# Opening of an attention and gated FFN kernel: another order, per-chunk loads, and pooling moved between TensorE and VectorE

## Chip, cores and metric

The kernel runs on one core of a Trainium2 chip. The metric is device microseconds of one execution; before the change three runs took 1026.32, 1027.2 and 1026.94 us (median 1026.94).

## What is computed

Four images (B = 4) of 384 x 32 positions and 128 channels. The reference pools kv by 4 x 4 pixels, projects it, attends to it with q, and sends the result through a gated feed-forward layer without biases:

```python
kv_pool = kv.reshape(B, H // r, r, W // r, r, C).mean(axis=(2, 4))   # r = 4
k = v = kv_pool.reshape(B, -1, C) @ w_sr                             # 768 keys an image
a = softmax(q @ k.T / sqrt(C))
x = (a @ v).reshape(B * S, D)                                        # 49152 rows of 128
out = (np.maximum(x @ w_gate, 0) * (x @ w_val)) @ w_out              # d_ff = 1536
```

## The kernel before

**Tiles and stages.** The rows of q are cut into 96 tiles of 512 (24 an image). An image has 768 pooled keys, in six chunks of 128. For each tile TensorE (PE) computes scores against the six chunks, ScalarE (ACT) their exponentials, PE the values, then for each of twelve blocks of 128 hidden columns a value projection and a gate projection, which ScalarE and VectorE (DVE) turn into one block of h, and an output projection. The softmax's row sums are applied last: since the layer has no bias, the output is scaled by the square of the reciprocal sums.

**Two parts in time.** The loop over k (L719) runs tiles through a pipeline, with the order of the engines' work written out by hand as lists of words: FIRST for the first two rounds, STEADY, DRAIN and LAST. Ahead of it stands the opening, the list OPENING (L70), which must pool and project image 0's keys, make the attention of tiles 0 to 3 and the hidden layer of tile 0. Nothing reorders the words: every engine gets its instructions in the order of the list, and waits where an operand or a buffer isn't ready.

**Words of the opening** (j is a chunk, k a tile, n a hidden block):

- a, b, c j (L628): add lines of chunk j's pixels, 128 x 512 fp32, as SUMS (L98) says: a adds two loaded lines, b and c add a third and fourth to the sum. p j (L632) halves the sum to 256 wide.
- T j.part (L637 to turn_add, L270): transposes on PE by an identity matrix, 128 x 128 each, all summed in one PSUM bank of chunk j. A loaded line (parts 0 to 3) has four, part p has two.
- kvT j (L276) copies that bank out, pj j (L284) projects it, key j (L286) stores keys, vt j (L295) and val j (L298) make and store their transpose, the values.
- cast k, qt k, qT k (L184, L190, L193): q tile k cast to fp16, transposed on PE, copied out. qT4 and qT5 are transposing DMAs on the SP queue (L197).
- S k.j (L344): scores of tile k against chunk j, and at once their exponential on ScalarE (L345), called E below. V k.j (L418): values added up in tile k's bank. xT k (L425): that bank copied out, once its six V are in.
- U, R (L432, L440): row sums of tiles 0 to 3 and their reciprocal and square; sixteen small GpSimd (POOL) copies spread the squares (L447).
- v n and g n (L455, L468): projections of tile 0, each followed at once by its consumer: the copy of the value (L462, called y) and the gating on VectorE (L476, called h), which multiplies the value by the positive part of the gate.
- gate, W, wo: GpSimd waits for a line, then starts the loads of the FFN weights; wo also loads the rest of q's second group.

ENGINES (L66) says on which engine a copy or add runs: a for ScalarE, p for GpSimd, else VectorE.

**PSUM banks** are handed out round about, eight in the opening and six for its last eight words; an operation that wants a bank waits for the last reader of that bank.

**Loads.** SP issues, in order (L592 to L600): chunks 0 and 1 (pair 0, four lines of 512 KB; ScalarE issues two of them), w_sr, q tiles 0 and 1, pair 1's line 0, q tiles 2 and 3, pair 1's other lines, pair 2's four lines (chunks 4 and 5), and q tiles 5 and 4 in four pieces of 64 KB each. Eight DMA semaphores go round: a DMA is issued when the one eight before it has landed.

**What opens the loop.** FIRST begins `r v1 o0 v8 v10 o1`: a value projection of tile 1, then the output projection of tile 0's hidden block 0 (o0, L496), which reads what h0.0 wrote. ScalarE's exponentials of the loop are L364; a-turns are transposing DMAs on SP (L391); GpSimd loads the next group of q after the opening (L699, L144). Before the first transposes PE runs a fill of five fp32 matmuls (L615, two passes each).

The functions that the change touches:

Of the kernel before, what the change touches and what calls it, by code (L numbers as in the profile page):

```python
# [9 lines left out]
FP32 = mybir.dt.float32  # L10
FP16 = mybir.dt.float16
AF = mybir.ActivationFunctionType
ALU = mybir.AluOpType
# [3 lines left out]
def kernel(  # L17
# [48 lines left out]
    ENGINES = dict(word.split(":") for word in """  # L66
        key0:a val0:a a1:p kvT1:a key1:a val1:a key2:a val2:a a3:p b3:p p3:p kvT3:a val3:a
        cast0:a cast1:a qT1:a cast3:a cast4:p cast5:p xT1:a xT3:a
    """.split())
    OPENING = """  # L70
        T0.1 T1.3 cast1 T0.3 cast0 T1.2 T0.2 a1 p1 T1.p T0.0 kvT1 kvT0 pj1 qt1 pj0 T2.0 qT1 a3
        key1 cast3 qt0 cast2 vt1 qT0 key0 S1.1 qt2 qt3 qT2 val1 qT3 S1.0 S0.1 T2.1 S0.0 vt0 val0
        V1.1 S2.0 b3 c3 S2.1 S3.0 S3.1 T2.2 V0.1 T2.3 V1.0 kvT2 V2.1 V0.0 p3 gate22 W0 W1 cast4
        qT4 wo cast5 qT5 pj2 V2.0 T3.p T5.0 key2 vt2 kvT3 val2 pj3 key3 S0.2 T5.1 vt3 val3 S2.3
        a4 S0.3 S1.2 S2.2 T5.2 V0.2 S3.2 b4 V2.3 T5.3 V0.3 c4 S1.3 kvT5 S3.3 pj5 p4 T4.p V1.2
        key5 kvT4 V1.3 S0.5 pj4 key4 S2.5 vt5 val5 V2.2 S0.4 vt4 val4 S2.4 V0.5 V3.0 S1.4 V0.4
        S3.4 xT0 S1.5 V2.5 V2.4 S3.5 xT2 v0.5 g0.5 U0 v0.2 U1 v0.0 R g0.2 v0.3 V1.4 V3.1 g0.0
        v0.1 v0.4 V1.5 g0.3 v0.9 v0.11 g0.4 g0.9 V3.4 v0.8 v0.10 g0.1 xT1 g0.8 V3.5 v0.7 g0.11
        V3.3 v0.6 V3.2 g0.10 xT3 g0.7 g0.6
    """.split()  # L80
    LAST = [f"{head}{n}" for n in range(NFB) for head in "ovygh"] + ["oT"]
    FIRST = """
# [14 lines left out]
    """.split()  # L97
    SUMS = [{}, {"a": [0, 1]}, {}, {"a": [0, 1], "b": ["s", 2], "c": ["s", 3]}, {"a": [0, 1], "b": ["s", 2], "c": ["s", 3]}, {}]  # L98

# [16 lines left out]
    def freed(ps):  # L116
        free_banks.append(bank_numbers.pop(id(ps))[0])
        return ps
# [90 lines left out]

    def kv_load(b, pair, lines=range(r), queues=(nc.sync,)):  # L210
# [12 lines left out]
        rows = kv[b, pair * 2 * HC : (pair + 1) * 2 * HC].rearrange(  # L223
            "(hp dh) (wp h dw) c -> dh hp wp (h dw c)", dh=r, h=2, dw=r
        )
        for dh in lines:
            queues[dh % len(queues)].dma_start(
                parts[dh].rearrange("p h dw c -> p (h dw c)"), rows[dh]
            )

# [16 lines left out]
    def line(chunk, dh):  # L247
        return kv_in[0, chunk // 2][dh][:, chunk % 2]
# [3 lines left out]
    def add(name, to, x, y):  # L252
        engine_of(name).tensor_tensor(to, x, y, op=ALU.add)
# [6 lines left out]
    def sum_pixels(name, chunk):  # L260
        s1 = sums.pop(chunk)
        pixels[chunk] = work.tile([128, 2, C], FP32, tag="kv_c2", bufs=2, name="kv_c2")
        add(name, pixels[chunk], s1[:, 0:2], s1[:, 2:4])

    def turn_add(chunk, lines):
# [72 lines left out]
    hTs, o_banks, o_sbs, vals = {}, {}, {}, {}  # L338

    def scores(k, jc):  # L340
        if k not in aTs:
            aTs[k] = work.tile([128, NJC, T], FP16, tag="aT", bufs=AT_BUFS, name="aT")
        s_ps = bank([128, T])
        nc.tensor.matmul(s_ps, kv16[:, k // NST, jc, 0:C], qT_of(k), start=True, stop=True)  # L344
        nc.scalar.activation(aTs[k][:, jc, :], freed(s_ps), AF.Exp, scale=qk_scale)  # L345

# [79 lines left out]

    def lead_sums(chunks):
        if "sums" not in x_banks:
            x_banks["sums"] = bank([128, T])
        for jc in chunks:  # L430
            for k in range(LEAD):
                nc.tensor.matmul(  # L432
                    x_banks["sums"][32 * k : 32 * (k + 1), :], ones, aTs[k][:, jc, :],
                    start=jc == 0, stop=jc == NJC - 1, skip_group_check=True,
                    tile_position=(0, 32 * k),
                )

    def lead_scales():
# [21 lines left out]
    def keep_value(k, fb):  # L460
        vals[k, fb] = work.tile([128, T], FP16, tag="val", bufs=6, name="val")
        (nc.vector.tensor_copy if k < LEAD - 1 and fb == 5 else nc.scalar.copy)(  # L462
            vals[k, fb], freed(proj_banks.pop(("v", k, fb)))
        )
# [125 lines left out]

    w_sr_f32 = const.tile([128, C], FP32)
    kv_load(0, 0, range(r), (nc.sync, nc.scalar))  # L592
    nc.sync.dma_start(w_sr_f32, w_sr)
    q_load_pair(0)
    kv_load(0, 1, range(1))
    q_load_pair(2)
    kv_load(0, 1, range(1, 4))
    kv_load(0, 2)
    q_load_tile(5)
    q_load_tile(4)  # L600

# [16 lines left out]

    fill(5)
    freed(idle)  # L620

    gate = const.tile([128, 1], FP32)
    done = set()

    def open_step(word):
        head = "T" if word[0] == "T" else word.rstrip("0123456789.")
        at = [int(x) for x in word[len(head):].split(".") if x] if head != "T" else []
        if head in ("a", "b", "c"):  # L628
# [5 lines left out]
        elif head == "r":  # L634
            c2 = pixels[at[0]]
            add(word, c2[:, 0], c2[:, 0], c2[:, 1])
        elif head == "T":  # L637
            j, part = word[1:].split(".")
            turn_add(
                int(j), line(int(j), int(part)) if part.isdigit() else  # L640
                pixels.pop(int(j))[:, 0 : 2 if part == "p" else 1],
            )
# [16 lines left out]
        elif head == "S":  # L659
            scores(*at)  # L660
            done.add(tuple(at))
        elif head == "V" and at[0] < LEAD:
# [3 lines left out]
        elif head == "U":  # L666
            lead_sums(range(at[0] * (NJC - 1), NJC - 1 + at[0]))
        elif head == "R":
            lead_scales()
        elif head == "v":  # L670
            value_proj(*at)
            keep_value(*at)
        elif head == "g":
            gate_proj(*at)
            gated(*at)
        elif head == "W":
# [19 lines left out]
    for at, word in enumerate(OPENING):  # L696
        usable[0] = 8 if at < len(OPENING) - 8 else 6
        open_step(word)
# [110 lines left out]
```

## Time and profile before

| | us |
|---|---|
| median of three runs | 1026.94 |
| span of the profiled execution | 1024.5 |
| PE busy | 1019.4 |
| ScalarE busy | 919.9 |
| VectorE busy | 861.8 |
| GpSimd busy | 524.8 |
| first transpose of pixels starts | 8.07 |
| first projection of keys starts (L284) | 11.69 |
| first and last exponential of the opening start | 13.77, 28.23 |
| first output matmul, o0 (L496), starts | 36.66 |

The span is that of one execution under the profiler, from its first to its last instruction; that execution's own time beyond the span isn't listed, so the median stands 2.4 us above it. Times below are counted from the span's start. A line of the timeline gives start, duration, engine, source line and operation, what it writes and reads, how many instructions were merged (x), and in brackets the engine's idle time before and what ended it.

### The profile page before, as it was taken

The page shows a single profiled execution, that of the slowest core. Times are in us where ns is not written, and L with a number is a line of the kernel's source. Part 1 is how long each engine was busy: PE and PEld are TensorE (multiplying, and loading weights), DVE is VectorE, ACT ScalarE, POOL GpSimd, SP SyncE. Part 2 cuts the span into 40 slices and gives each one's busy share as a digit, 9 for nine tenths or more (in the row PEclk, how much of TensorE's full clock was granted, in tenths as well). Part 3 has the DMA queues.
Part 4 walks back from the last instruction along what each step waited for, and adds up shares of the span by engine and source line. Part 5 has one row for each costly group of instructions (what it writes and reads, how often), then busy time and mean ns, then how long its engine had stood idle before and what let it go on. Part 6 is the DMA issues. An engine that isn't in the chain of part 4 may idle for free.

```text
span 1024.5 us, 17514 instructions
## 1 busy us (share of the span) xinstructions
PE 1019.4 (100%) x5048; PEld 489.5 (48%) x5048; DVE 861.8 (84%) x1432; ACT 919.9 (90%) x1931; POOL 524.8 (51%) x1308
## 2 busy tenths in 40 slices
PE   9999999999999999999999999999999999999998
PEld 5444444444444444444444444444444444444445
DVE  2888888888888888888888888888888888888888
ACT  5999999989999999899999999989999999999986
POOL 3588857344346586544434856654333543343342
DMA  9999999877998999869879899887686987867541
GB/s 330 159 173 184 176 183 159 151 131 120 139 184 168 189 186 164 143 115 146 128 126 211 160 180 194 157 138 134 118 139 108 145 134 119 129 115 123 102 87 45
DMA packets 475312, 153.49 MB, mean 150 GB/s; under 512 B 451536, under 2 KB 465360, under 8 KB 475216
## 3 DMA queue, kind: packets, MB, share of 16 engines
q1 hardware_dynamic: 453184, 126.08, 67.7%
q0 software_dynamic: 21600, 25.19, 15.9%
q10 hardware_dynamic: 432, 1.11, 0.3%
q8 instruction: 40, 0.66, 0.3%
q14 instruction: 56, 0.46, 0.1%
HBM read 53.94 MB, written 26.35 MB: 78 GB/s over the span
## 4 chain that ended last, share of the span: by engine, by line
PE 98%; DMA 1%; ACT 1%; SPq 0%; issue 0%
PE bank_ps L455 24%; PE bank_ps L468 24%; PE bank_ps L496 23%; PE bank_ps L401 12%; PE wide_ps L359 12%; DMA q<-in_q_dram 1%; PE bank_ps L482 1%; PE bank_ps L344 1%; PE bank_ps L418 1%; PE bank_ps L270 0%; PE wide_ps L302 0%; PE bank_ps L284 0%; ACT a L364 0%; ACT val L462 0%; PE bank_ps L432 0%
## 5 line engine op out<-in xcount | busy, mean ns | idle before, releaser
L476 DVE SCALAR_TENSOR_TENSOR hT<-bank_ps,val 128x512 f16<-128x512 f32 x1152 | 727.8, 680 | 105.4 <-PE bank_ps L468 83.7
L462 ACT CAST val<-bank_ps 128x512 f16<-128x512 f32 x1149 | 628.1, 595 | 45.4 <-PE bank_ps L455 24.9
L455 PE MATMUL bank_ps<-xT,wv 128*128 128x512 f16 x1152 | 420.5, 379 | 0.0
L468 PE MATMUL bank_ps<-xT,wg 128*128 128x512 f16 x1152 | 375.9, 379 | 0.0
L496 PE MATMUL bank_ps<-hT,wo 128*128 128x512 f16 x1116 | 348.4, 379 | 0.0
L364 ACT ACTIVATE a<-wide_ps 128x768 f16<-128x768 f32 x368 | 302.0, 821 | 44.0 <-PE wide_ps L359 43.9
L359 PE MATMUL wide_ps<-kv,qT 128*128 128x512 f16 x736 | 179.7, 326 | 0.1
L401 PE MATMUL bank_ps<-aT,kv 128*128 128x512 f16 x552 | 178.9, 379 | 0.0
L496 PEld LDWEIGHTS <-wo 128*128 128x128 f16 x1116 | 109.2, 98 | 131.9 <-issue 0.6
L468 PEld LDWEIGHTS <-wg 128*128 128x128 f16 x1152 | 112.7, 98 | 122.4 <-issue 0.2
L509 POOL TENSOR_TENSOR o_sb<-o_t,scale 128x512 f32<-128x512 f32 x89 | 93.2, 1047 | 145.9 <-issue 128.4
L455 PEld LDWEIGHTS <-wv 128*128 128x128 f16 x1152 | 112.7, 98 | 105.7 <-issue 1.2
L385 POOL COPY scale<-square 32x8 f32<-32x8 f32 x736 | 141.2, 192 | 28.6
L739 POOL DMA_DIRECT2D out_dram<-o_sb x216 | 134.8, 627 | 19.5 <-POOL o_sb L509 13.0
L378 POOL TENSOR_TENSOR square<-inverse 128x8 f32<-128x8 f32 x46 | 9.3, 202 | 255.6 <-DVE inverse L376 249.4
L359 PEld LDWEIGHTS <-qT 128*128 128x128 f16 x736 | 72.0, 98 | 87.1 <-issue 0.4
L409 DVE CAST xT<-bank_ps 128x512 f16<-128x512 f32 x92 | 63.6, 691 | 32.0 <-PE bank_ps L401 32.0
L401 PEld LDWEIGHTS <-kv 128*128 128x128 f16 x552 | 54.0, 98 | 65.1
L364 ACT ACTIVATION_READ_ACCUMULATOR a<-wide_ps 128x1 f32 x368 | 75.9, 206 | 0.0
L504 DVE STREAM_TRANSPOSE o_t<-bank_ps 128x512 f32<-128x512 f32 x93 | 65.4, 703 | 0.0
L144 POOL DMA_DIRECT2D q<-in_q_dram x84 | 46.7, 573 | 0.6 <-PE bank_ps L496 0.4
L237 POOL TENSOR_TENSOR s<-kv_in 128x512 f32<-128x512 f32 x36 | 45.1, 1284 | 0.7
(78 smaller groups left out, 204.9 us busy)
## 6 DMA issues: line engine op xcount, KB each, us to landing
kv_in<-in_kv_dram SPq DMA_DIRECT2D x42, 512.0 KB, 4.7
out_dram<-o_sb SPq DMA_DIRECT2D x177, 64.0 KB, 3.7
out_dram<-o_sb POOLq DMA_DIRECT2D x176, 64.0 KB, 4.2
q<-in_q_dram POOLq DMA_DIRECT2D x84, 128.0 KB, 5.8
aT<-a SPq DMA_TRANSPOSE x184, 4.3
kv_line<-in_kv_dram SPq DMA_DIRECT2D x4, 512.0 KB, 9.7
placed<-blocks SPq DMA_DIRECT2D x9, 128.0 KB, 2.7
kvT<-placed SPq DMA_DIRECT2D x36, 32.0 KB, 2.1
```

What stands on the lines that cost most here:

```text
L359: nc.tensor.matmul(s_ps[:, j0 * 128 : j1 * 128], qT, kv16[:, b, j0:j1, 0:C], start=True, stop=True)
L364: nc.scalar.activation(a16s[k][:, s, :], s_banks.pop(s)[:, 0:J], AF.Exp, scale=qk_scale, accum_out=a_sums[k // 2][:, k % 2, s : s + 1],)
L385: nc.gpsimd.tensor_copy(to[32 * b : 32 * (b + 1), :, :, j], squares[k // 2][32 * j : 32 * (j + 1)])
L401: nc.tensor.matmul(x_banks[k], kv16[:, k // NST, jc, C : 2 * C], aT[:, jc], start=first, stop=x_left[k] == 0,)
L455: nc.tensor.matmul(proj_banks["v", k, fb], wv16[:, fb * 128 : (fb + 1) * 128], xTs[k], start=True, stop=True,)
L462: (nc.vector.tensor_copy if k < LEAD - 1 and fb == 5 else nc.scalar.copy)(vals[k, fb], freed(proj_banks.pop(("v", k, fb))))
L468: nc.tensor.matmul(proj_banks["g", k, fb], wg16[:, fb * 128 : (fb + 1) * 128], xTs[k], start=True, stop=True,)
L476: nc.vector.scalar_tensor_tensor(hTs[k][:, fb, :], freed(proj_banks.pop(("g", k, fb))), 0.0, vals.pop((k, fb)), op0=ALU.max, op1=ALU.mult,)
L496: nc.tensor.matmul(o_banks[k], wo16[:, fb, :], hTs[k][:, fb, :], start=fb == 0, stop=fb == NFB - 1)
L504: nc.vector.transpose(o_t, freed(o_banks.pop(k)))
L509: nc.gpsimd.tensor_tensor(to, o_by, scale.to_broadcast([128, NS, 4, 32]), op=ALU.mult)
L739: queue.dma_start(*out_moves.pop())
```

## The change

Only the opening is changed; FIRST, STEADY, DRAIN and LAST stay.

1. **Loads.** The order is a list, LOADS. It is the same up to pair 2, whose four lines become eight loads of 256 KB: first chunk 4's half of each line, then chunk 5's.
2. **Pooling.** A new word, d j.part, sums the four neighbouring pixels of a line or of a sum with one tensor_reduce on VectorE (512 to 128 wide). Chunks 0 and 3 are wholly added up (a, b, c) and reduced; PE then has a single transpose for each (T j.ds). Chunk 4 has its line 2 and its sum of lines 0 and 1 reduced (d2, ds) and line 3 transposed. Chunk 1's sum goes to PE unreduced (T1.s). In all PE has 36 such transposes instead of 62.
3. **Order.** Scores and exponentials, projections and their consumers are words of their own (S and E, v and y, g and h), and the list is written anew. The row sums U come in one run near the end, R after them; cast4, qT4, wo, cast5 and qT5 stand just before R. The list ends with `R g0.4 y0.4 h0.4 h0.0`.
4. **Smaller things.** Other engines for some copies and adds; the square of R on GpSimd; the value copy that VectorE takes for tile 0 is block 2's; the fill has three matmuls; six banks hold for the last twelve words.

```diff
+        a0 a1 T1.s b0 T1.2 T1.3 kvT1 c0 pj1 cast1 cast0 d0.s key1 qt1 qt0 qT1 T0.ds vt1 kvT0
+        qT0 S1.1 pj0 val1 E1.1 S0.1 key0 cast3 V1.1 E0.1 vt0 cast2 S0.0 qt3 val0 E0.0 V0.1 qt2
+        a2 S1.0 qT3 V0.0 qT2 a3 S3.0 S3.1 E3.0 p2 S2.0 T2.2 b3 E3.1 T2.p S2.1 E2.0 T2.3 c3 E2.1
+        V3.1 E1.0 V2.0 kvT2 V2.1 d3.s pj2 V1.0 a4 V3.0 key2 T3.ds vt2 S0.2 kvT3 S3.2 val2 E0.2
+        pj3 d4.2 S2.2 key3 T4.3 d4.s E3.2 T4.d2 S1.3 E2.2 T4.ds vt3 V3.2 a5 kvT4 gate21 W0 W1
+        V0.2 E1.3 S3.3 pj4 val3 V2.2 E3.3 b5 V1.3 S2.3 key4 S0.3 p5 vt4 E2.3 T5.3 E0.3 T5.p
+        S1.4 V2.3 kvT5 val4 S2.4 E1.4 pj5 S0.4 E2.4 V0.3 key5 V1.4 E0.4 S0.5 S2.5 vt5 E0.5 V2.4
+        S1.5 val5 V0.4 E2.5 V0.5 S3.5 E1.5 S3.4 xT0 V2.5 E3.5 S1.2 V1.5 xT2 v0.2 E1.2 v0.5 v0.3
+        y0.2 E3.4 g0.2 g0.5 y0.5 V3.5 h0.2 V3.4 v0.1 y0.3 v0.11 h0.5 g0.3 y0.1 g0.1 v0.10 h0.3
+        y0.11 g0.10 g0.11 V1.2 h0.1 y0.10 v0.6 g0.9 xT1 h0.11 g0.6 v0.9 y0.6 V3.3 h0.10 v0.7
+        y0.9 v0.8 v0.0 h0.6 g0.7 y0.8 g0.8 h0.9 y0.7 U1 U4 U3 y0.0 h0.8 U2 U0 xT3 U5 h0.7 v0.4
+        g0.0 cast4 qT4 wo cast5 qT5 R g0.4 y0.4 h0.4 h0.0
...
+    LOADS = "P0 w Q0 P1.0 Q2 P1.1 P1.2 P1.3 K4 K5 q5 q4".split()
...
+            if half is not None:
+                own = slice(half * r * C, (half + 1) * r * C)
+                to, line_rows = to[:, own], line_rows[:, :, own]
...
+    def reduce_pixels(chunk, part):
+        lines = sums.pop(chunk) if part == "s" else line(chunk, int(part))
+        reduced[chunk, part] = work.tile([128, 1, C], FP32, tag="kv_d", bufs=4, name="kv_d")
+        nc.vector.tensor_reduce(
+            reduced[chunk, part][:, 0], lines.rearrange("p w c -> p c w"),
+            axis=mybir.AxisListType.X, op=ALU.add,
+        )
...
-        nc.scalar.activation(aTs[k][:, jc, :], freed(s_ps), AF.Exp, scale=qk_scale)
+
+    def exponentials(k, jc):
+        nc.scalar.activation(
+            aTs[k][:, jc, :], freed(score_ps.pop((k, jc))), AF.Exp, scale=qk_scale
+        )
...
-        nc.vector.tensor_tensor(square, inverse, inverse, op=ALU.mult)
+        nc.gpsimd.tensor_tensor(square, inverse, inverse, op=ALU.mult)
...
-    fill(5)
+    fill(3)
```

On GpSimd are now b0, a4, cast0, cast2, cast4 and cast5; on ScalarE cast1, kvT0, kvT4, key0 to key4, val4, qT2, qT3, xT1 and xT3; the rest of such words on VectorE.

More of the change, by code (lines that the diff above doesn't have):

```diff
@@ L73 @@
[L73 to L78, printed above, removed]
@@ L208, with kv_load @@
     kv_in = {}
-    def kv_load(b, pair, lines=range(r), queues=(nc.sync,)):
+    def kv_load(b, pair, lines=range(r), queues=(nc.sync,), half=None):
         if (b, pair) not in kv_in:
@@ L425, in lead_kept, with lead_sums @@
         copy_on(name, xTs[k], freed(x_banks.pop(k)))
-    def lead_sums(chunks):
+    def lead_sums(jc):
         if "sums" not in x_banks:
[L429 to L436, printed above, removed]
+            x_banks["sums"], x_count["sums"] = bank([128, T]), 0
+        x_count["sums"] += 1
+        for k in range(LEAD):
+            nc.tensor.matmul(
+                x_banks["sums"][32 * k : 32 * (k + 1), :], ones, aTs[k][:, jc, :],
+                start=x_count["sums"] == 1, stop=x_count["sums"] == NJC, skip_group_check=True,
+                tile_position=(0, 32 * k),
+            )
     def lead_scales():
@@ L636, in open_step @@
             add(word, c2[:, 0], c2[:, 0], c2[:, 1])
+        elif head == "d":
+            j, part = word[1:].split(".")
+            reduce_pixels(int(j), part)
         elif head == "T":
@@ L640, in open_step @@
                 int(j), line(int(j), int(part)) if part.isdigit() else
+                sums.pop(int(j)) if part == "s" else
+                reduced.pop((int(j), part[1:])) if part[0] == "d" else
                 pixels.pop(int(j))[:, 0 : 2 if part == "p" else 1],
@@ L660, in open_step @@
             scores(*at)
-            done.add(tuple(at))
+        elif head == "E":
+            exponentials(*at)
         elif head == "V" and at[0] < LEAD:
```

61 lines of the change are left out of this document (30 added, 31 removed).

## Prediction

> **What bounds the kernel now.** I read the chain of waits first, then the busy time after the opening, then PE, ScalarE and VectorE in order of time up to 38 us.
>
> ```profile
> PE 98%; DMA 1%; ACT 1%; SPq 0%; issue 0%
> ```
>
> The chain that ends last is matmuls nearly from end to end. In the windows view (PE's busy time is the second number), the stretch from 36.70 us on reads:
>
> ```profile
> 36.70:1024.50 987.80, 984.48 (x4846) 469.55 (x4844) 845.38 (x1397) 895.76 (x1880) 508.88 (x1267) 1.00 0.84 146
> ```
>
> Matmuls there start 0.216 us apart (512 columns); only twice does one start over 0.1 us late, 0.27 us at 54.8 and 0.18 at 424.7. So the loop has 0.45 us to give back, and the end moves with the first output matmul o0 (L496), which opens it:
>
> ```profile
> 36.44 0.38 PE L455 MATMUL bank_ps<-xT,wv 128*128 128x512 f16 x1
> 36.66 0.38 PE L496 MATMUL bank_ps<-hT,wo 128*128 128x512 f16 x1
> ```
>
> What o0 needs is made by VectorE (first fence) and ScalarE (second), here from about 25 us:
>
> ```profile
> 26.96 0.69 DVE L128 CAST xT<-bank_ps 128x512 f16<-128x512 f32 x1 [0.85 <-PE bank_ps L418]
> 27.83 0.69 DVE L128 CAST xT<-bank_ps 128x512 f16<-128x512 f32 x1 [0.17 <-PE bank_ps L418]
> 28.43 0.68 DVE L462 CAST val<-bank_ps 128x512 f16<-128x512 f32 x1
> 29.23 0.69 DVE L476 SCALAR_TENSOR_TENSOR hT<-bank_ps,val 128x512 f16<-128x512 f32 x1
> 30.36 0.72 DVE L440 STREAM_TRANSPOSE sums_turned<-bank_ps 128x512 f32<-128x512 f32 x1 [0.44 <-PE bank_ps L432]
> 31.11 0.25 DVE L442 RECIPROCAL inverse<-sums_turned 128x16 f32<-128x16 f32 x1
> 31.49 6.69 DVE L476 SCALAR_TENSOR_TENSOR hT<-bank_ps,val 128x512 f16<-128x512 f32 x11
> ```
>
> ```profile
> 20.72 3.76 ACT L345 ACTIVATE aT<-bank_ps 128x512 f16<-128x512 f32 x7
> 24.83 4.05 ACT L345 ACTIVATE aT<-bank_ps 128x512 f16<-128x512 f32 x8 [0.34 <-PE bank_ps L344]
> 29.99 1.73 ACT L462 CAST val<-bank_ps 128x512 f16<-128x512 f32 x3 [1.12 <-PE bank_ps L455]
> ```
>
> VectorE ends its twelve gatings at 38.18, 1.5 us after o0, without harm: h0.0, the one that o0 reads, was early in the list. ScalarE ends its exponentials at 28.87, then idles 1.12 us while PE runs row sums. The first question is where the new list puts h0.0.
>
> **The change, part by part.** Pitches from rows (start to start): an exponential or a value copy on ScalarE 0.48, a small ScalarE copy 0.17, gating on VectorE 0.60, a 512-wide fp32 add on VectorE 0.69 (0.72 when it needs the one before), a 128-wide copy there 0.29, a transpose group of four 0.44 plus 0.17 to its result.
>
> *Loads.* Eleven DMAs up to the second pair's last line are issued as before; that line is issued at 8.67 and lands 8.0 later, 16.7. Then four 512 KB loads become eight of 256 KB, 2 KB a partition. SP issues each when the DMA eight before has landed, the last at 16.7, so SP isn't late. The last full line landed at 22.2:
>
> ```profile
> kv_line<-in_kv_dram SPq DMA_DIRECT2D x1, 512.0 KB, 10.6
> ```
>
> Price: 512 KB landed every 1.28 us before it, so 2 MB at that pace ends at 21.85. The nearest 2 KB row is the late q loads (64 KB, 32 partitions): five land from 22.45 to 23.43, 0.245 us each; at that rate a half takes 0.98 us and the eighth lands at 24.6. I take 22.2: same source and same 128 partitions as the full lines. The Trainium skill, DMA: Bandwidth & Descriptors, section Specifications, asks only 512 B a transfer for line rate, which would give 21.85; the q row disagrees, and no run shows halves yet. Behind the halves on SP the late q loads are issued from about 17.4 on (12.9 before), but the last of the eight waits, as before, for the last line, 22.2: so cast4 (27.17), wo (issued 27.73, landed 33.17) and qT4 stay, all before o0. Without that cover, o0 would wait for wo one for one.
>
> *PE.* Transposes fall from 62 to 36: 26 x 0.109 = 2.8 us less. Of the fill, four of ten passes go (0.43 each); the first transposes then wait for two adds on VectorE after line 0 (landed 6.22), 7.7 instead of 8.07. PE is nearly idle from 6.4 to 11. The fill's passes are 0.85 us apart until 5.8 and 0.43 after; should half rate return, PE's 2.4 us of work from 10.3 to 14.3 runs some 0.9 late, which ScalarE's idle spots below (1.3 us by 19.2) take up. I cost it at nothing; without that cover it is the 0.9.
>
> *VectorE.* It has four wide adds now; it gets nine and four reductions: 5 x 0.69 + 4 x 0.69 = 6.2 us more, put into its long waits (3.27, 2.14, 2.00 us before its L128, L253 and L291 instructions). A reduction of 512 to 128 isn't in the trace: at least the 0.43 of a 512-wide cast between buffers, at most the 1.27 of GpSimd's add. I take 0.69, as the adds, which read as many elements on this engine. The Trainium skill, VectorE: DVE Perf Modes, section The perf-mode tier table, has it at one element a cycle in every type, like the fp32 add; by that the sum is the one below, by the cast's row it is rival (2), and no run here shows it yet.
>
> **The new path to o0.** From 16.7 VectorE carries one chain: c3 0.72, kvT2 0.31, reduction d3 0.70, out to PE and back 0.35, kvT3 0.29, val2 0.25, reductions d4.2 and d4.s 0.72 each, 0.05 of semaphore: 4.1, so 20.8. T4.ds on PE and its wait, 0.35: ScalarE starts kvT4 at 21.2. Ahead of E0.5 ScalarE has three small copies (0.51), seven exponentials (3.36) and about 0.3 of waits for scores: E0.5 runs 25.36 to 25.95. PE sums V0.5 (0.53 with V0.4 in front), and xT0 starts at 26.5, 0.46 earlier than now. ScalarE starts exponentials 1.2 us sooner (12.6 against 13.77), but that is lost: it idles 0.5 and 0.76 us between 17.7 and 19.2 and 0.33 before kvT4.
>
> From xT0 VectorE has two xT and y0.2 (3 x 0.61), twelve gatings (12 x 0.60), the row sums' transpose and reciprocal (1.04; the square goes to GpSimd), 0.3 for y0.2's result and the last one's tail: 10.4. ScalarE is no longer in its way: its value copies run from 28.3 (29.99 now), the 1.12 us gap is gone, and all end by 35.2. So VectorE ends at 36.9 against 38.18. But h0.0 is now the last of the list, behind the row sums: o0, second in the loop's list, waits for it until 36.95. PE, done with the opening at about 34.9, stands for 2 us.
>
> **Sum:** 36.95 - 36.66 = +0.3 us. Backlogs of ScalarE and VectorE at o0 are smaller, which can return at most the 0.27 at 54.8; I leave it. Span 1024.8 against 1024.5. The median of the runs shown lies 2.4 above that span; same offset: **1027.2 us**, no change that counts. (A measurement of this kernel tells about 0.2%, 2.05 us, from no change.)
>
> The sums' late place also moves GpSimd: its sixteen scale copies (31.64 to 35.29 now) run from 35.8 to 39.6 and hold the next q load (issued 37.08, last landing 44.15 now) to 39.9, landing about 47.0. SP's transpose of it starts at 48.24 now; 1.2 us of cover hide it. Gone, that transpose would hold the stores and a-turns behind it on SP.
>
> **Rivals.** (1) *Slower: the halves land late.* T5.3, the last line's transpose, stands in PE's queue from 22.8, with S1.4, V2.3 and all later matmuls behind it. A last half later than 22.8 delays everything one for one; at 24.6, 1.8 us: +2.1, **1029.1**. For: the q row. Against: 32 partitions aren't 128, and full lines ran 1.28 us to the end.
> (2) *A little faster.* Reductions at 0.43 shorten the chain by 3 x 0.26; T5.3 then waits for the landing: -0.6 on the path, **1026.6**. The floor is the landing at 21.85 with nothing else late: T5.3 and T5.p (0.85), kvT5 (0.35), pj5 (0.45), key5 (0.3) and S0.5 (0.45) put E0.5 at about 24.25, 1.1 earlier, and o0 at 35.8: **1026.1**. Over 2 us isn't in reach.
> (3) *Reductions at 1.27*, by their strided read: 3 x 0.58 = +1.7, **1028.9**.
> (4) *It doesn't do what it says:* chunks 0 and 3 do reach PE as one transpose each; that fewer transposes buy nothing is the forecast itself.
>
> **How the numbers follow.** Forecast 0.57, (1) 0.17, (2) 0.14, (3) 0.07, a wait that I missed 0.05. The range takes in the bounds of the unknown prices, with some 0.2 below the floor for the runs' own spread (0.9 here): 1025.9 to 1029.1. Slower by over 0.2% (above 1029.0) is half of (1), half of (3) and the missed waits: 0.17. Faster: 0.03. Same: 0.80.
>
> **What would show it.** VectorE's reductions at 0.69; the last half landing by 22.2 to 22.8; xT0 near 26.5; ScalarE going from exponentials to value copies without a gap; the last opening gating ending at about 36.9, and PE idle some 2 us just before the first output matmul. Wrong if that matmul starts clearly before 36, if the loop shows stalls that it lacks now, or if 512-wide matmuls still stand 0.43 us apart past 16 us.

## The result, and the profile after

| us | before | after |
|---|---|---|
| median of 20 runs | 1026.81 | 1028.38 |
| lowest and highest of them | 1026.23, 1027.56 | 1027.31, 1034.09 |
| span of the profiled execution | 1024.5 | 1032.3 |
| first output matmul, o0, starts | 36.66 | 37.76 |
| from o0 to the end of the span | 987.9 | 994.5 |

The ratio is 1.002, 95% interval 1.0013 to 1.0026: the changed kernel is about 0.2% slower. The forecast was 1027.2, in a range of 1025.9 to 1029.1. The median lies in the range and 1.2 us above the forecast, and the new runs are spread over 6.8 us where the old ones had 1.3. So there are two questions: why o0 starts later than forecast, and where the spread comes from. The profiled execution is the slowest of the 20 (1034.09 us) and shows both.

The chain of waits of the changed kernel, which was 98% PE and 1% DMA:

```profile
PE 94%; DMA 4%; DVE 1%; ACT 1%; issue 0%; DVEq 0%
```

The stretch from o0 on, in the windows view (columns: stretch, its length, then busy time and count of PE, its weight loads, VectorE, ScalarE and GpSimd; then clock, DMA share, GB/s):

```profile
37.76:1032.30 994.54, 986.33 (x4845) 469.90 (x4844) 844.56 (x1394) 896.15 (x1878) 511.49 (x1280) 1.00 0.84 145
```

Before, this stretch took 987.80 with 984.48 of it busy. Here it has 6.7 us more, so most of this execution's loss lies *behind* the opening that was changed. PE in order of time shows two waits in it, each in front of a value product (L423) for a transposed block of exponentials that a DMA on SP brings:

```profile
114.22 0.38 PE L477 MATMUL bank_ps<-xT,wv 128*128 128x512 f16 x1
115.94 0.38 PE L423 MATMUL bank_ps<-aT,kv 128*128 128x512 f16 x1 [1.33 <-DMA aT<-a]
...
178.77 0.38 PE L477 MATMUL bank_ps<-xT,wv 128*128 128x512 f16 x1
182.45 0.59 PE L423 MATMUL bank_ps<-aT,kv 128*128 128x512 f16 x1 [3.30 <-DMA aT<-a]
```

The idle time in brackets counts from the modelled end of the matmul before, so what is lost is the distance of the starts less 0.216: 1.5 and 3.5 us. The second wait is followed by 3.42 us at half the clock, which costs 1.7 more:

```profile
182.44:185.86 3.42, 3.41 (x9) 1.33 (x10) 1.38 (x2) 1.34 (x3) 0.00 (x0) 0.50 1.46 170
```

1.5 + 3.5 + 1.7 = 6.7, all that the stretch has more. The other new executions that were profiled and have no such wait take 987.7 to 988.1 us from o0 to the end, as before. So the time of each profiled run here is the start of o0 plus the waits in the loop, and I follow the two apart.

**The opening.** PE at o0 (first fence; before, o0 followed the projection ahead of it without a gap), then VectorE from the landing of pair 1's last line (16.90) to o0, then ScalarE:

```profile
36.01 0.38 PE L477 MATMUL bank_ps<-xT,wv 128*128 128x512 f16 x1
37.76 0.38 PE L519 MATMUL bank_ps<-hT,wo 128*128 128x512 f16 x1 [1.37 <-DVE hT L499]
```

```profile
16.99 0.69 DVE L259 TENSOR_TENSOR kv_s<-kv_s,kv_in 128x512 f32<-128x512 f32 x1 [0.40 <-DMA kv_in<-in_kv_dram]
17.69 0.29 DVE L132 COPY kvT_chunk<-bank_ps 128x128 f32<-128x128 f32 x1
17.90 1.03 DVE L276 TENSOR_REDUCE kv_d<-kv_s 128x128 f32<-128x512 f32 x1
...
19.70 1.04 DVE L276 TENSOR_REDUCE kv_d<-kv_line 128x128 f32<-128x512 f32 x1
20.65 1.02 DVE L276 TENSOR_REDUCE kv_d<-kv_s 128x128 f32<-128x512 f32 x1
...
27.48 1.34 DVE L132 CAST xT<-bank_ps 128x512 f16<-128x512 f32 x2 [0.64 <-PE bank_ps L440]
28.77 0.69 DVE L485 CAST val<-bank_ps 128x512 f16<-128x512 f32 x1
29.58 6.08 DVE L499 SCALAR_TENSOR_TENSOR hT<-bank_ps,val 128x512 f16<-128x512 f32 x10
35.58 0.71 DVE L462 STREAM_TRANSPOSE sums_turned<-bank_ps 128x512 f32<-128x512 f32 x1
36.32 0.25 DVE L464 RECIPROCAL inverse<-sums_turned 128x16 f32<-128x16 f32 x1
36.49 1.22 DVE L499 SCALAR_TENSOR_TENSOR hT<-bank_ps,val 128x512 f16<-128x512 f32 x2
```

```profile
22.16 0.27 ACT L130 COPY kvT_chunk<-bank_ps 128x128 f32<-128x128 f32 x1 [0.68 <-PE bank_ps L311]
...
24.82 4.61 ACT L365 ACTIVATE aT<-bank_ps 128x512 f16<-128x512 f32 x9
29.31 2.06 ACT L485 CAST val<-bank_ps 128x512 f16<-128x512 f32 x4
```

This is the forecast's chain with another number in it. o0 waits for the gating that is last in the list (ends at 37.71), ScalarE goes from exponentials to value copies without a gap, and the row sums stand between the last gatings. But each reduction takes 1.02 to 1.04 us, where the forecast had 0.69, and kvT4 (22.16 against 21.2), xT0 (27.48 against 26.5) and o0 (37.76 against 36.95) are late by 0.96, 0.98 and 0.81. The line that starts the chain is late too: it landed at 16.90 (forecast 16.7).

Seven of the eight halves landed from 17.57 on, 0.67 to 0.69 apart, and the last 1.27 behind the seventh, at 22.91:

```profile
kv_line<-in_kv_dram SPq DMA_DIRECT2D x8, 256.0 KB, 7.5
```

PE turned the last of them (T5.3) at 23.74; it did not wait for it.

### The profile page after: what moved, and what is told of

It is laid out like the page before. It is cut to its first block, busy times and chain, and to the rows that moved or that the text cites. A ratio compares the mean times of both kernels' runs of the same rounds, so it can differ in the third digit from the quotient of the medians.

```text
span 1032.3 us, 17469 instructions
## 1 busy us (share of the span) xinstructions
PE 1017.6 (99%) x5018; PEld 485.7 (47%) x5018; DVE 868.5 (84%) x1440; ACT 920.6 (89%) x1929; POOL 525.1 (51%) x1309
## 3 DMA queue, kind: packets, MB, share of 16 engines
q10 hardware_dynamic: 432, 1.11, 0.3%
## 4 chain that ended last, share of the span: by engine, by line
PE 94%; DMA 4%; DVE 1%; ACT 1%; issue 0%; DVEq 0%
PE bank_ps L477 24%; PE bank_ps L491 24%; PE bank_ps L519 23%; PE bank_ps L423 12%; PE wide_ps L381 11%; DMA aT<-a 2%; DMA kv_in<-in_kv_dram 1%; PE bank_ps L505 1%; DMA kv_line<-in_kv_dram 1%; DVE hT L499 1%; PE wide_ps L318 0%; PE bank_ps L440 0%; ACT a L386 0%; PE bank_ps L362 0%; ACT val L485 0%
## 5 line engine op out<-in xcount | busy, mean ns | idle before, releaser
L423 PE MATMUL bank_ps<-aT,kv 128*128 128x512 f16 x552 | 179.7, 381 | 4.6 <-DMA aT<-a 4.6
L423 PEld LDWEIGHTS <-kv 128*128 128x128 f16 x552 | 54.2, 98 | 71.1 <-issue 6.7
```

What stands on the lines that cost most here:

```text
L423: nc.tensor.matmul(x_banks[k], kv16[:, k // NST, jc, C : 2 * C], aT[:, jc], start=first, stop=x_left[k] == 0,)
```

## The experiments

**Theory** after reading the two traces: (a) the reductions make o0 about 0.9 us late; (b) the fill of three matmuls instead of five lets TensorE's clock fall back to half in the opening of many executions; (c) the loop's waits come from the late load of q's third group on GpSimd (issued at 41.19, before 37.08) and from SP's in-order transpose of it (49.58, before 48.24). **Rivals:** the halves, or the order of the words, make o0 late; the waits follow from the half clock, or from something in the opening that neither (b) nor (c) names.

How to read the times of many runs, of which only one is profiled: a stretch of 3.41 us at half clock lowers the mean clock of a run by 0.5 x 3.41/1024 = 0.0017, so 0.998 is one such stretch, 0.997 or 0.996 two. As a mark for a wait in the loop I count the runs that lie over 2.0 us above the fastest of the same kernel; half clock in the opening alone made less (e1). It is a mark and no proof: the wait itself is seen only in a profile, a short wait goes unmarked, and e10's two marked runs are just the longest of its five at a clock of 0.998.

| kernel | median, us | lowest, highest | runs with the mark |
|---|---|---|---|
| changed (all above) | 1028.38 | 1027.31, 1034.09 | 2 of 20 |
| e1 changed, again | 1028.88 | 1027.27, 1033.73 | 4 of 10 |
| e2 fill of five | 1027.47 | 1027.19, 1027.86 | 0 of 11 |
| e3 blocks renamed | 1029.36 | 1025.76, 1033.62 | 9 of 12 |
| e4 adds for reductions | 1027.11 | 1026.37, 1034.06 | 1 of 12 |
| e5 renamed, fill of five | 1026.16 | 1025.85, 1030.73 | 2 of 12 |
| e6 as e5, q early | 1025.98 | 1025.82, 1026.42 | 0 of 12 |
| e7 before, fill of three | 1027.17 | 1026.33, 1033.55 | 1 of 12 |
| e8 before, q late | 1027.43 | 1026.24, 1034.71 | 5 of 12 |
| e9 changed, q early | 1030.14 | 1027.42, 1034.04 | 6 of 12 |
| e10 as e6, whole lines | 1027.90 | 1027.09, 1029.38 | 2 of 12 |
| e11 as e6, adds | 1025.43 | 1025.18, 1028.97 | 1 of 12 |
| e12 as e9, fill of five | 1027.62 | 1027.19, 1029.32 | 1 of 11 |
| before, beside e1 to e4 | 1026.85 | 1026.11, 1027.37 | 0 of 33 |
| before, beside e5 to e8 | 1026.84 | 1026.12, 1033.74 | 3 of 35 |
| before, beside e9 to e11 | 1026.83 | 1026.22, 1032.37 | 2 of 29 |
| before, beside e12 | 1026.82 | 1026.28, 1027.43 | 0 of 15 |

The four groups of experiments (e1 to e4, e5 to e8, e9 to e11, e12) ran on different chips, so a kernel is best compared within its group.

### e1: the changed kernel again

> The changed kernel once more, unaltered, for a second profile and for the spread. Theory A (half clock): the runs that are longest by 0.8 to 1.6 us are those whose mean granted clock is under 0.999, since PE now stands nearly idle between about 6 and 11 us; in a profile of such a run the 512-wide matmuls of the opening stand 0.43 us apart for one or two stretches of 3.4 us. Theory B (loop stalls): the long runs are long because a transposing load of the attention weights lands late in the loop, as at 178 us of the first profile, and any half clock comes after such a stall. Both expect a median of about 1028.4; A expects the fastest runs, at clock 1.000, near 1027.4.

Measured: ratio 1.0029 (1.0017 to 1.0042). This profiled execution has no wait in the loop (987.93 us from o0 to the end) but another opening: o0 at 38.64, 0.88 later than in the first profile. The windows view has the reason, the clock (the column behind the engines):

```profile
5.00:7.60 2.60, 0.59 (x2) 0.00 (x0) 1.07 (x2) 0.00 (x0) 0.00 (x0) 1.00 1.03 424
7.60:11.01 3.41, 2.98 (x12) 2.28 (x12) 0.23 (x1) 0.48 (x1) 1.72 (x2) 0.50 1.03 407
```

The same stretch of the first profile, without the half clock:

```profile
7.60:11.01 3.41, 2.22 (x14) 1.57 (x14) 1.01 (x3) 0.50 (x1) 1.74 (x2) 1.00 1.04 410
```

PE has 14 matmuls in 2.22 us of busy time there; at half clock it is through with 12 in 2.98. So kvT1, the copy behind the first transposes, waits longer on VectorE (first profile, then e1), and the sums, scores and exponentials behind it start later:

```profile
10.19 0.29 DVE L132 COPY kvT_chunk<-bank_ps 128x128 f32<-128x128 f32 x1 [2.40 <-PE bank_ps L286]
11.15 0.29 DVE L132 COPY kvT_chunk<-bank_ps 128x128 f32<-128x128 f32 x1 [3.32 <-PE bank_ps L286]
```

The delay reaches o0 whole: xT0 28.36 against 27.48. A late load is not the reason, since pair 1's last line landed at 16.91, and at 16.90 in the first profile. Counted from that landing, the opening's last gating ends after 20.81 to 20.83 us in the five profiles with halves, reductions and full clock (the first, e5, e6, e9, e12), after 21.67 in e1 and 21.55 in e3, the two with half clock; e2 (21.33) has one add of 1.11 us instead of 0.69.

Of the changed kernel's 20 runs, 11 had a clock of 0.998 or less, in one of them (the profiled one) from the stretch behind the loop's wait; the two marked runs left out, those at 0.996 took 1028.99 to 1029.28, those at 0.998 1028.22 to 1028.37, and the lowest at 0.999 or more 1027.31 to 1027.56: some 0.85 us for each stretch. (None with two was profiled. Three unmarked runs at full clock took 1027.96, 1028.40 and 1029.20; what held them isn't known.) The Trainium skill, TensorE: Matmul & The Clock Gate, section What's actually happening, has a window of 3413 ns for the gate that runs free of the kernel, so that the time of a change of clock differs between runs of one kernel; the 3.41 us and the spread agree.

### e2: the fill at five

```diff
-    fill(3)
+    fill(5)
```

> The changed kernel with the fill of before (five matmuls instead of three). Theory A (half clock in the opening): PE is kept busy until about 7.5 us, hardly any run is under clock 0.999, and the median falls by about 0.8 us to 1027.6, with a narrower spread. Theory B (loop stalls): median and spread stay as in the changed kernel, 1028.4 and some 2 us.

Measured: 1027.47, ratio 1.0006 (0.9998 to 1.0015), clock 1.000 or 0.999 in all 11 runs, no mark. So the two matmuls of fill are worth 1.4 us of the median (e1 beside it: 1028.88). In the forecast they were costed at nothing. (The profile's own o0, 38.16, is late by the long add; e12, with the same opening, has 37.51.) The fill covers the hole: with it, PE is busy in the whole of 5.00 to 7.60 (here in e12, whose opening is the same on PE), where e1 had 0.59 us.

```profile
5.00:7.60 2.60, 2.60 (x7) 0.91 (x5) 1.29 (x2) 0.00 (x0) 0.00 (x0) 1.00 1.02 414
```

The traces' clock records change at steps of 3.41 us: in the first profile, 52 of them back from 182.44 is 4.95, and e1's stand at 4.18, 7.60 and 11.01. PE's busy time in the step around the hole, in the first profile and in e1:

```profile
4.95:8.36 3.41, 1.53 (x7) 0.61 (x5) 1.29 (x2) 0.00 (x0) 0.00 (x0) 1.00 1.02 414
4.19:7.60 3.41, 1.40 (x4) 0.32 (x2) 1.07 (x2) 0.00 (x0) 0.00 (x0) 1.00 1.03 423
```

With three matmuls, the next step was at half clock after 1.40, 1.55 and 1.30 us of work (e1, e3, e7) and not after 1.53, 1.75 and 1.84 (the first profile, e4, e9); with five, no step of the profiled openings between 4 and 14 us has under 2.2. So the short fill leaves a step near an edge, which these traces don't place more sharply. Where the steps lie differs from run to run, so a run can go either way: of all stretches of 3.41 us there, the emptiest has 0.98 to 1.75 us of work in the profiles of the new order with three matmuls, and 2.03 or more in those with five (worked out from PE's rows).

### e3: the block that o0 reads is gated first

The blocks of tile 0 are only renamed (2 and 0 change places, and others), so each engine has the same work at the same place:

```diff
-        ... v0.2 E1.2 v0.5 v0.3 y0.2 E3.4 g0.2 ... h0.2 ... R g0.4 y0.4 h0.4 h0.0
+        ... v0.0 E1.2 v0.1 v0.2 y0.0 E3.4 g0.0 ... h0.0 ... R g0.10 y0.10 h0.10 h0.11
```

> The changed kernel with the hidden blocks of tile 0 renamed in the opening, so that the same instructions stand in the same places but the block that the loop's first output matmul reads is the first that VectorE gates and not the last. Theory A (the first output matmul waits for the last gating): that matmul starts right behind the value projection ahead of it, at about 36.2 us instead of 37.8, PE's idle time of 1.4 us there goes, and the time falls by 1.5 us, below the kernel before the change. Theory B (the late path through exponentials and VectorE sets the loop's start whatever block comes last): PE meets the same wait a few matmuls later and the time falls by less than 0.4 us.

Measured: in the profile o0 starts at 36.63, right behind the projection ahead of it, while the last gating ends at 38.11; from o0 on 988.06 us. With the order of the changed kernel o0 would have stood till 38.11 (this execution has half clock from 8.94 to 12.35): the last place of h0.0 costs 1.5 us. It is the forecast's reading of the list, confirmed. In time the lowest run shows it, 1025.76 against 1027.27 in e1. But the median became *longer*, 1029.36, since 9 of 12 runs have the mark. Four of these nine ran at a clock of 1.000, so half clock is no condition of the waits.

### e4: two adds for each reduction

```diff
-        nc.vector.tensor_reduce(reduced..., lines.rearrange("p w c -> p c w"), axis=X, op=add)
+        nc.vector.tensor_tensor(half, lines[:, 0:2], lines[:, 2:4], op=ALU.add)
+        nc.vector.tensor_tensor(reduced..., half[:, 0], half[:, 1], op=ALU.add)
```

> The changed kernel with each tensor_reduce (1.04 us in its profile) replaced by two adds on VectorE, 512 to 256 and 256 to 128 wide, which the profile's rows put at 0.43 and 0.29. Theory A (three of the four reductions stand in the one chain that leads to the loop): each gives 0.32 us, the first xT starts about 0.9 us sooner (26.6 instead of 27.5), and the time falls by 0.8 to 0.9 us, where the landing of the last half line (22.9) begins to bind. Theory B (the exponentials on ScalarE set the start of the first xT): xT moves by less than 0.3 us and the time with it.

Measured: 1027.11, ratio 1.0009 (0.9998 to 1.002). What follows a pair of adds starts 0.72 and 0.66 us after the pair's start (19.42, 20.14, 20.80), about what the forecast had for a reduction; behind the reductions it was 0.95 and 0.94:

```profile
19.42 0.47 DVE L276 TENSOR_TENSOR kv_d<-kv_line 128x256 f32<-128x256 f32 x1
19.93 0.29 DVE L278 TENSOR_TENSOR kv_d<-kv_d 128x128 f32<-128x128 f32 x1
20.14 0.42 DVE L276 TENSOR_TENSOR kv_d<-kv_s 128x256 f32<-128x256 f32 x1
20.59 0.29 DVE L278 TENSOR_TENSOR kv_d<-kv_d 128x128 f32<-128x128 f32 x1
20.80 0.69 DVE L259 TENSOR_TENSOR kv_s<-kv_line 128x512 f32<-128x512 f32 x1
```

and o0 comes out where the forecast put it, 36.96 (forecast 36.95), with the landing that the forecast had for pair 1's last line (16.71), xT0 at 26.68 (26.5) and the same wait in front:

```profile
36.96 0.38 PE L518 MATMUL bank_ps<-hT,wo 128*128 128x512 f16 x1 [1.36 <-DVE hT L498]
```

### e5 and e6: both mends, and then the load of q early

e5 is e3 with the fill at five. e6 is e5 with this:

```diff
-        ... cast5 qT5 R g0.10 y0.10 h0.10 h0.11
+        ... cast5 qT5 q2 R g0.10 y0.10 h0.10 h0.11
...
+        elif head == "q":
+            nc.gpsimd.tensor_copy(gate, hTs[0][:, 9, 0:1])
+            q_load(at[0])
...
-    nc.gpsimd.tensor_copy(gate, hTs[0][:, NFB - 1, 0:1])
-    q_load(2)
```

> The changed kernel with two edits: the blocks of tile 0 renamed so that the block that o0 reads is gated first (as in the run before, alone), and the fill back at five matmuls. Theory (reductions at 1.04 us cost about 0.9, the half clock of the opening another 0.8 in most runs, and waits in the loop come from the late load of q's third group, which here waits for the gating that ends last): no half clock in the opening, o0 at 36.2 to 36.8, clock 1.000 in nearly all runs; but the load of q is issued no earlier than 41.5, so waits in the loop stay in some of the runs, 1026.0 to 1026.6 in those without one and up to several us more in those with one. Rival (the waits in the loop come from the half clock in the opening): none in any run, all within 1026.0 to 1026.8.

> As the kernel before it in this call, and the load of q's third group is issued before the sixteen scale copies on GpSimd, behind the gating of block 9 instead of block 11. Theory: the load is issued at 36 to 37.5 and lands by about 44.5, SP's transpose of it starts at about 48.3 without holding anything, no run has a wait in the loop: 1025.8 to 1026.5 in all runs. Rival (the load of q has nothing to do with it): the spread over runs is that of the kernel before it in this call. A second rival (the scale copies are now late for the first scaling of an output): a wait in the loop near 45 to 50 us in every run, longer by up to 2 us.

Measured: e5 1026.16, e6 1025.98 (ratio 0.9981, 0.9965 to 0.9998). The clock was 0.999 or 1.000 in all runs but one of e5. In e6 the load is issued at 36.30 (e5 40.99), its last part lands at 45.13 (50.82), and SP's transpose starts at 47.97 (50.97). e5 has two marked runs and e6 none, which is too few to tell them apart; the second rival, scale copies late for the first output, is out (988.07 us from o0 on). In e6, o0 follows the projection ahead of it at once:

```profile
35.96 0.38 PE L477 MATMUL bank_ps<-xT,wv 128*128 128x512 f16 x1
36.17 0.38 PE L519 MATMUL bank_ps<-hT,wo 128*128 128x512 f16 x1
```

### e7: the kernel before, with the short fill

> The kernel before the change, with a fill of three matmuls instead of five and nothing else. Theory (the shorter fill lets the clock fall back to half for 3.4 us somewhere between 6 and 14 us, and this is on the path): granted clock 0.996 to 0.998 in more than half of the runs, these 0.5 to 1.6 us longer than before; the ones at 1.000 within 0.3 us of it; median 1027.3 to 1028. Rival (before's many transposes, 62 of them, keep PE busy enough, so that the short fill harms only together with the smaller number of transposes): clock 1.000 and 1026.5 to 1027.2 throughout. What I had costed: nothing.

Measured: 1027.17. The theory's "more than half of the runs" is wrong: 3 of 12 had a clock of 0.998 or less, against 11 of 20 and 8 of 10 with the new order. The profile is one of the three, with half clock from 8.86 on and o0 at 37.78 instead of 36.66; so the short fill can harm the old order too, but seldom. The old list has 26 transposes of pixels on PE ahead of its first projection of keys, the new one 12 (T1.s, T1.2, T1.3), behind two adds.

### e8: the kernel before, with the load of q late

```diff
-    nc.gpsimd.tensor_copy(gate, hTs[0][:, NFB - 1, 0:1])
+    nc.gpsimd.tensor_copy(gate, hTs[0][:, 6, 0:1])
+    spread_squares(squares.pop("lead"))
     q_load(2)
```

(spread_squares holds the sixteen copies, which stood in lead_scales.)

> The kernel before the change, with its sixteen scale copies and the load of q's third group behind the gating of block 6, the last one (ends 38.18), nothing else: the load is issued at about 41.8 instead of 37.08, as in the changed kernel; o0 and the clock of the opening stay as they are. Theory (late load, in-order transpose on SP, late a-turns, waits in the loop): the load lands at about 48.5 to 50, SP's transpose of it starts 1 to 2 us later than 48.24, the least slack of the a-turns of tiles 5 to 15 falls under 4.6 us, and some of the runs, a third or more, are over 1028 with waits between 50 and 200 us. Rival (the late load is harmless): 1026.2 to 1027.4 in all runs, as before.

Measured: the load is issued at 42.74 and lands at 52.23, and SP's transpose waits for it, with the stores and a-turns behind it (columns: start, time that SP stood at the instruction, what it moves):

```profile
46.89 2.39 SPq L391 DMA_TRANSPOSE aT<-a  x1
52.37 1.23 SPq L155 DMA_TRANSPOSE qT<-q  x1
53.70 0.79 SPq L743 DMA_DIRECT2D out_dram<-o_sb  x1
```

Before, it was issued at 48.24, and SP had not stood ahead of it. Five of 12 runs have the mark, against 3 of 35 of the kernel before beside it; the least slack of an a-turn (landing to the values that read it) is 1.32 us, before 4.63. So a late load (with the scale copies, which the edit moves too) seems to be able to bring waits into the loop. The slack alone doesn't sort the kernels: in the other profiles without a wait it is 2.18 (e3) to 5.83 (e2), and 2.34 in e11. o0 was at 37.38 in this execution though its opening is the old one. Pair 2's last line landed at 22.70 instead of 22.22 and xT0 started 0.47 later; the other 0.25 was not followed. One profile's o0 is good to some 0.7 us.

### e9 and e12: the changed kernel with the load of q early; then with the fill at five

e9 has the edit of e6 (behind the gating of block 7) on the changed kernel; e12 has fill(5) besides.

> The changed kernel with one edit: the load of q's third group is issued ahead of the sixteen scale copies, behind the gating of block 7, at 36 to 37.5 instead of 41.2 to 42. Theory (the late load causes the waits in the loop, the short fill the half clock of the opening): the waits in the loop go in all or all but one of the runs, so none is over 1029.5; the half clock stays in more than half of the runs; 1027.3 to 1029.2, median about 1028.3. Rival (the waits in the loop follow from the half clock): several runs over 1029.5, as in the changed kernel.

> The kernel with the early load of q, which had waits in the loop in most of its runs although that load was early, with the fill at five matmuls instead of three and nothing else. If the short fill goes with the waits (0 of 11 runs of the changed kernel had one with five matmuls): clock 0.999 or 1.000 and 1027.1 to 1027.9 in all runs or all but one. If they come from something that the fill doesn't touch, as the distance between o0 and the load of q: several runs over 1029, as with three.

Measured: e9 1030.14, ratio 1.0032 (1.0017 to 1.0047), 6 of 12 marked. The load was early (36.35, its transpose at 49.43), and still in the profiled execution PE waits twice for an a-turn, till 157.94 and 182.03, 1.6 and 2.9 us beyond the pitch. That refutes (c) as *the* cause in the changed kernel. e12 took 1027.62, clock 0.999 or 1.000, 1 of 11 marked. So two matmuls of fill take most of the waits away: 4 of 10 to 0 of 11 (e1, e2), 9 of 12 to 2 of 12 (e3, e5), 6 of 12 to 1 of 11 (e9, e12), three pairs in one direction. Of these, only the first ran on one chip. In all, with the new order, 22 of 66 runs with three matmuls have the mark and 6 of 70 with five; but with three the kernels differ among themselves, from 1 of 12 (e4) and 2 of 20 (the result) to 9 of 12 (e3).

### e10: whole lines again

```diff
-    LOADS = "... P1.3 K4 K5 q5 q4".split()
+    LOADS = "... P1.3 P2 q5 q4".split()
```

> The kernel with renamed blocks, five matmuls of fill and the early load of q, and pair 2 loaded again as four whole lines of 512 KB instead of eight halves. Line 3 then lands at about 22.2 for both chunks, while its transposes for chunk 4 stood on PE at 20.23 with the halves. If the halves are what brings chunk 4 forward: the last transpose of chunk 4 at about 22.9 instead of 21.69, o0 0.9 to 1.2 us later, 1026.9 to 1027.2. Rival (T5.3 and the last line's landing set the end with either): 1025.9 to 1026.3, no change.

Measured: 1027.90 against e6's 1025.98; o0 37.46 against 36.17, +1.29. With whole lines, line 3's transposes for chunk 4 stand till the last line is there (22.10), 2.06 us with PE idle; with halves (e6) they ran at 20.23:

```profile
19.80 0.38 PE L362 MATMUL bank_ps<-qT,kv 128*128 128x512 f16 x1
22.24 0.63 PE L286 MATMUL bank_ps<-ident,kv_line 128*128 128x128 f32 x4 [2.06 <-DMA kv_line<-in_kv_dram]
```

The halves gain 1.3 us, and the rival (the last landing sets the end either way) is out. Five runs had a clock of 0.998, though the fill has five matmuls; whether it fell in this hole was not profiled. (A step of 3.41 us that holds the whole hole has 3.41 - 2.06 = 1.35 us of work, an estimate.) They lift the median over the 1026.9 to 1027.2 that was expected; six of the seven others took 1027.09 to 1027.52.

### e11: all that helped

e6 with e4's adds.

> All that helped together: renamed blocks, five matmuls of fill, early load of q, and each tensor_reduce replaced by two adds. Theory: clock 1.000 everywhere, no waits in the loop, o0 at 35.2 to 35.5, 1024.9 to 1025.6 in all runs, 1.3 to 1.8 us less than before. Rival (with cheaper sums the last half's landing, 22.4 to 22.9, holds T5.3 instead): o0 at 35.7 to 36.2, no gain over 1025.98, which is what the kernel with the reductions took.

Measured: 1025.43, ratio 0.9988 (0.9979 to 0.9997), 1.4 us less than the kernel before, clock 1.000 in all runs, one marked run. o0 at 35.56 follows PE's projections without a gap, 0.61 earlier than in e6; a little less than the theory's 0.7 to 1.0. The last half landed at 22.95 and T5.3 ran at 23.07, so the landing is next in line.

## Why the prediction was right in its range, and where it was not

1. **The end moves with o0.** Right: 987.7 to 988.1 us from o0 on in all profiled executions without a wait in the loop. (The reading "only twice" missed a third late start, 0.17 at 37.04, right behind o0.)
2. **o0 waits for h0.0, the last word of the list.** Right: o0 37.76, last gating 37.71, PE idle 1.37 us (forecast some 2); e3 shows 1.5 us for the place.
3. **Halves land in time.** Right, though not at 22.2: 22.91 in this profile, 22.41 to 22.95 elsewhere. PE came to T5.3 later than forecast as well (22.95 at the earliest, forecast 22.8), so it never waited. The 0.67 us for a half is near the pace of the full lines (0.64), not that of the late q loads (0.98), so rival (1) fell; only the last half took 1.08 to 1.41. That halves gain 1.3 us against lines (e10) is in the forecast's chain, where T4.3 doesn't wait, but was not named.
4. **"I take 0.69, as the adds."** Mis-sized: 1.02 to 1.04. This is most of what moved o0: with 0.72 (e4) o0 is at 36.96, the forecast's number, and with reductions at 37.76. Of the three in the chain, one is waited for to its end (1.04 - 0.70), one delays the next (0.95 - 0.72) and the last both (1.02 - 0.71): 0.34 + 0.23 + 0.31 = 0.88 was due. Of the 0.80 between the two profiles, 0.19 is the later landing of pair 1's last line (16.90, e4 16.71); counted from it, the reductions cost 0.61, and o0 moves by 0.61 between e6 and e11 too, where that line landed at 16.84 in both. Behind d3, part of the 0.88 goes into a longer wait for PE (0.60 us with adds, 0.42 with reductions). In time it is 0.90 between the lowest runs of e1 and e4, and 0.55 between the medians of e6 and e11. It is rival (3), between its price of 1.27 and the forecast. The Trainium skill, VectorE: DVE Perf Modes, section The perf-mode tier table, puts a reduction and an fp32 add at one element a cycle; here, with the four pixels 512 bytes apart, the reduction took half as long again as an add over as many elements, so the measurement decides. Whether the distance or the operation makes the difference, no run tells.
5. **"I cost it at nothing"**, of the fill: wrong. The step saw the half clock and its 0.9 us ("without that cover it is the 0.9"), and its size was right, 0.85; what failed is the cover. ScalarE's idle spots did not take the delay up, since what they wait for is late as well: kvT1 by 0.96, chunk 0's reduction by 0.87, and the two spots are as long in e1 (0.20 and 0.72 us) as in the first profile (0.19 and 0.70). xT0 and o0 are late by all of 0.88. By their clock, 10 of 20 runs had it, some twice.
6. **"1.2 us of cover hide it"**, of the late load of q: it was issued at 41.19, not 39.9, and landed at 48.33, not 47.0; SP's transpose stood at 49.58, so 1.25 of cover were left in this execution. It isn't sure: in e3, e5 and e8 the landing took till 51.26, 50.82 and 52.23 and the transpose was held to 51.41, 50.97 and 52.37. What the step says of that case ("would hold the stores and a-turns behind it on SP") is what e8 shows. But in the changed kernel the waits stay without it (e9), so it is not the cause of the spread.
7. **Waits in the loop** were no case of the forecast, which named them only as a sign of being wrong. Each one profiled is PE waiting for an a-turn of tiles 9 to 15. The resource behind it is SP's queue. An a-turn can be issued when ScalarE has the exponentials; counted from there, SP is through with its issue 4.3 to 12.5 us later in the kernel before (tiles 5 to 16), 1.5 to 12.0 in e1, up to 14.6 in e8 and 15.7 in e3 and e5, and in the two profiles with waits up to 19.0 (changed) and 18.1 (e9). The lag is built up by single issues at which SP stands, and handed on from tile to tile. In the changed kernel's profile the first of them are these, after which SP lags 8.5 us where it lagged 4.7 before:

```profile
49.58 3.18 SPq L159 DMA_TRANSPOSE qT<-q  x1
...
55.28 4.99 SPq L413 DMA_TRANSPOSE aT<-a  x1
```

In the kernel before these two took 1.31 and 3.30 us (at 48.24 and 52.29). Then comes one of 8.02 us at 101.56 (before: 6.94 at 93.96), while q's next loads are under way: the a-turn behind it was issued at 110.32, and PE waited for it until 115.94. So it is a weak spot of the loop that is not new; 5 of the old kernel's 112 runs beside the experiments have the mark too. **What stays open** is why openings with the short fill meet it more often. The three pairs point that way (two of them across chips), and the marked runs at full clock in e3 show that half clock in the opening is no condition. One profile doesn't tell: the lag was 12.0 in e1 and 15.1 in e11, and e1's runs have more marks. Nor does the trace tell what SP stands for at these issues; the releaser that it names, a value copy on ScalarE, has nothing to do with an a-turn.

The sum for a run at full clock without a wait is 36.66 + 0.3 (forecast) + 0.2 (landing) + 0.6 (reductions) = 37.76. In time it is less, since the profiled execution of the kernel before is one of its shortest: its span of 1024.5 goes with a time of 1026.3 in the runs beside the experiments, 1.8 more and not the 2.4 that the forecast added, and the kernel's median is 1026.81. The changed kernel's five lowest runs took 1027.31 to 1027.56, some 0.7 more than that median and within 0.4 of the forecast. The rest of the 1.2 us between forecast and median is half clock, in 10 of 20 runs, and the waits of a few. That the median still lies in the range is in part luck: the range was drawn for late halves and dear reductions, and half clock and waits in the loop had no share in its bounds.

## What to carry to other kernels

Price a reduction over a strided axis from a measurement or bound it by the whole range; two adds of contiguous halves did the same sum in 0.7 us instead of 0.95. Filler work in front of a sparse start can be on the path of every engine behind TensorE (0.85 us here): before it is cut, look at how busy TensorE is in the microseconds that follow, and judge by the clock of many runs, not by one profile. Before two profiles' stretches are compared, count both from the landing that starts them; here 0.19 of 0.80 us was the load. And where the last place in a hand-written list is what the next stage reads first, a renaming alone gives the wait back (1.5 us here).

## What the runs showed of the hardware

- A VectorE reduction from 128 x 512 to 128 x 128 fp32, over pixels 512 bytes apart, took 1.02 to 1.06 us in all profiles; a 512-wide fp32 add 0.69 (one of 1.11 in e2).
- The clock can fall to half again, for 3.41 us, after it had been full; in the step of 3.41 us ahead PE was busy for 1.30 to 1.55 us in the three profiles that show it in the opening (e1, e3, e7). It stayed full after steps with 1.53 (first profile), 1.75 (e4) and 1.84 (e9). The first profile has a stretch of 3.41 us across two steps with 0.98 us of work, and kept its clock there.
- Loads of 256 KB in pieces of 2 KB a partition landed every 0.675 us, 388 GB/s, all but the last of eight (the full lines: 512 KB every 1.28 us, 410 GB/s); the late q loads of 64 KB over 32 partitions had 267 GB/s.
- A transposing DMA on SP lands 4.6 to 4.8 us after its start in the median, and three of four within 6.1 us; the longest took 12.7 (first profile, at 94.56), with loads of q and kv and stores under way beside it. SP stood up to 8.3 us at the issue of one (e9, at 128.53).
